# Attention with a transposed probability ring: order of the next head's reads, and which two tiles TensorE transposes

## The chip, the cores and the metric

The kernel runs on one core of one Trainium2 chip. The metric is the device time of one execution in microseconds. A core has TensorE (PE; its weight loads are listed apart as PEld), VectorE (DVE), ScalarE (ACT), GpSimd (POOL) and SyncE (SP). SP computes nothing here: it issues almost all DMA transfers, one after the other in the order of its own program. Sixteen DMA engines carry them.

## The reference

An adaLN-conditioned block: cached multi-head attention, then a small mixer and MLP. Only the attention is touched by the change. There are 32 heads of width 128, 2048 queries and 2048 keys, model width 640, all in bf16.

```python
def _A_ref(x, k_cache, v_cache, wq, wo):
    q = (x @ wq).reshape(B, Sq, H, Dh).transpose(0, 2, 1, 3)
    scores = jnp.einsum('bhqd,bhkd->bhqk', q, k_cache) * Dh ** (-0.5)
    p = _softmax(scores, axis=-1)
    o = jnp.einsum('bhqk,bhkd->bhqd', p, v_cache)
    return o.transpose(0, 2, 1, 3).reshape(B, Sq, H * Dh) @ wo

h = _layernorm(x) * (1 + ca) + sa
x = x + ga * _A_ref(h, A_k_cache, A_v_cache, A_wq, A_wo)
h = _layernorm(x) * (1 + cb) + sb
x = x + gb * _B_ref(h, B_w1, B_w2, B_w3, B_w4)
```

## The kernel before, in words

**Stages.** A start loads x, normalises it and makes its transpose `hT` in SBUF. The attention follows, one head after the other. The block's output projection, mixer and MLP come last; the change does not touch them.

**Tiles and steps.** A head's 2048 queries are 16 tiles of 128 rows. Tiles are numbered through all heads, g = 16 h + j, and one loop (L532) goes over steps s, one tile a step, with several stages of different tiles in one step. A tile meets these:

- Scores, `qk`, on PE (L286): two halves of 1024 keys, each of two matmuls, into the two halves of `Sps` in PSUM. A half can be written again only when DVE has read it.
- `negS` on DVE (L574): each half is scaled and copied to SBUF, with its row minimum. Two a tile.
- The exponential on ACT (L587), into slot s % 10 of the ring `Pb`. POOL (L584) joins the two minima before it.
- The transpose of the 128 x 2048 probabilities, so that keys lie on partitions, into `PTs`, also ten slots. It is done in one of two ways, below.
- The product with V, `pv`, on PE (L299), eight steps later (`PVD = 8`): two halves of eight matmuls. A half needs its half of `PTs`. After every second tile ACT copies the result (L565), POOL divides by the row sum and stores it to `o_scratch` by its own queue (L454).

**The two transposes.** Most tiles go through a DMA transpose from SP (`transpose`, L220 to L224): issued behind the exponential of an odd tile for a pair of tiles (1 MB), or for a tile alone (0.5 MB) where its neighbour isn't transposed so. Two tiles of each head, `PE_TILES`, are transposed on PE against an identity instead (`t_piece`, L253): four 128 x 128 pieces at a time, two halves r of eight pieces, into one of two PSUM banks (`JB`, in `Oaug` and `QPp`); then a copy to `PTs` (`t_evac`) by ACT (L262) or DVE (L264), as `by_dve` says. Half r of tile g is transposed in step g + 3 + r. With `PE_TILES = (3, 10)` the DMA transposes of a head are (0,1), 2, (4,5), (6,7), (8,9), 11, (12,13), (14,15).

**Projections.** The queries of head h + 1 are made during head h: four chunks of five matmuls (`q_piece`, L237), one matmul in a half-step, in the same two PSUM banks, each chunk copied by ACT (L244). `QPIECE` puts the chunks into half-steps that `taken` leaves free of transposing pieces; before, at half-steps 0 to 9 and 16 to 25 of 32.

**Order on PE in a step.** For each half: `qk`, then `pv` of tile s - 8, then a projection matmul or a transposing piece. PE works in this order, as every engine does in its own; waits are semaphores, worked out by the class `Prog` from what is read and written.

**Order on ACT and DVE in a step.** ACT: the copy of a pair's result, the copies of projections and of transposed halves, then the exponential. DVE: two `negS`, then a transposed half, where `by_dve` gives it one.

**Order on SP.** Behind a step's transpose come the reads for the following heads, into buffers that alternate by head: `load_k` (L205, a DMA transpose from the cache) at tile 2, `load_wq` (L209) at tile 6 for two heads on, `load_v` (L214) at tile 9. V's buffer for head h + 1 was last read by `pv` of the head before h, whose last tile is worked on in step 7 of head h. In the last head two reads of `o_scratch` (`load_ot`) for the output projection stand at tiles 2 and 9 instead.

Of the kernel before, what the change touches and what calls it, by code (L numbers as in the profile page):

```python
# [115 lines left out]
def bass_adaLN_cond__mha_block_cached__mixer_s_mlp__prompt_kernel(  # L116
# [3 lines left out]
    _, H, SK, DH = A_k_cache.shape  # L120
# [3 lines left out]
    NQT = SQ // 128  # L124
# [7 lines left out]
    NG = H * NQT  # L132
# [5 lines left out]
    with ExitStack() as es:  # L138
# [11 lines left out]
        if True:  # L150
            with ExitStack() as es1:
                sb1 = lambda name, shape, dt: es1.enter_context(nc.sbuf_tensor(name, shape, dt))
                RP = 10
                PVD = 8
                PE_TILES = (3, 10)
                US = KT * (SQ + 4)
                sb1("pad", [128, 32], F32)
                ring = sb1("ring", [128, 2 * RP, SK], BF16)
# [44 lines left out]
                def load_k(h):  # L203
                    hb = h % 2
                    G.dma("sync", lambda e: e.dma_start_transpose(KTs[:, hb], A_k_cache[0, h]), ("k", hb), w=[("KT", hb)])  # L205

                def load_wq(h):
                    hb = h % 2
                    G.dma("sync", lambda e: e.dma_start(wq[:, hb], A_wq[:, h * 128:(h + 1) * 128].rearrange("(k p) d -> p k d", p=128)),  # L209
                          ("wq", hb), w=[("wq", hb)])  # L210

                def load_v(h):
                    hb = h % 2
                    G.dma("sync", lambda e: e.dma_start(Vaug[:, hb, :, 0:128], A_v_cache[0, h].rearrange("(t p) d -> p t d", p=128)),  # L214
                          ("v", hb), w=[("V", hb)])

                assert RP % 2 == 0 and NQT % 2 == 0
                is_pe = lambda g: g % NQT in PE_TILES

# [8 lines left out]
                def bank(key):  # L228
                    if key not in bank_of:
                        bank_of[key] = jbank[0] % 2  # L230
                        jbank[0] += 1
                    return bank_of[key]
# [14 lines left out]
                def t_piece(g, r, q):  # L247
                    jb = bank(("t", g, r))

                    def f(t):  # L250
                        for z in range(4 * q, 4 * q + 4):
                            kt = 8 * r + z
                            ins = t.transpose(JBb[jb][:, z * 128:(z + 1) * 128], Pb[:, g % RP, kt * 128:(kt + 1) * 128], ident[:])  # L253
                        return ins
                    G.op("tensor", f, r=[("Pb", g % RP)], w=[("J", jb)])
# [7 lines left out]
                    else:  # L263
                        G.op("vector", lambda v: v.tensor_copy(dst, src), r=[("J", jb)], w=[("PT", g % RP, r)])  # L264

                by_dve = lambda g, r: r == 1 and g % NQT == PE_TILES[0]

                taken = [u for j in PE_TILES for u in range(2 * (j + 3), 2 * (j + 5))]
                QPIECE = {}
                u = 0  # L270
                for cc in range(NQC):
# [60 lines left out]
                if H > 1:  # L332
# [8 lines left out]
                     r=["id0"], w=["ident"])  # L341
# [3 lines left out]
                for k in range(KT):  # L345
                    G.op("gpsimd", lambda g, k=k: g.tensor_scalar(out=s_bc[:, k, :], in0=ones_f, scalar1=c_f[:, k:k + 1],
                                                                  scalar2=1.0, op0=ALU.mult, op1=ALU.mult),
                         r=["onesf", "cf"] + WRK, w=[("sbc", k)])
# [52 lines left out]
                def q_head0(cc):  # L401
                    for q in range(KT):
                        q_piece(0, cc, q)
                    q_evac(0, cc)
# [127 lines left out]
                for s in range(NG + PVD + LAG):  # L532
                    h, j = divmod(s, NQT)
                    g_ = s - PVD
                    evacs = []
                    if s <= 2:
                        for i in ((0,), (1, 2), range(3, len(MROW)))[s]:
                            mod_rows(i)
                    if s == 3:
                        G.op("gpsimd", lambda g: g.tensor_scalar(  # L540
                            out=mod_bc[:, 2 * D:3 * D], in0=mod_bc[:, 2 * D:3 * D], scalar1=1.0, scalar2=1.0, op0=ALU.add, op1=ALU.mult),
                            r=[("mod", i) for i in range(len(MROW))], w=["mod"])
                    for half in range(2):
                        if s < NG:
                            qk(s, half)
                        if half == 0 and s in (NG + PVD - 3, NG + PVD - 2):
                            b0 = a_pe(0, None if s == NG + PVD - 3 else b0, (s - NG - PVD + 3,))
                        if 0 <= g_ < NG:
                            pv(g_, half)
                        if s == 0 and half == 1:  # L550
                            q_head0(NQC - 1)
                        if h + 1 < H and 2 * j + half in QPIECE:
                            cc, q = QPIECE[2 * j + half]
                            q_piece(h + 1, cc, q)
                            if q == KT - 1:
                                evacs.append((q_evac, h + 1, cc))
                        for r in range(2):
                            g = s - 3 - r
                            if 0 <= g < NG and is_pe(g):
                                t_piece(g, r, half)  # L560
                                if half == 1:
                                    evacs.append((t_evac, g, r))
                    if 0 <= g_ < NG and g_ % 2 == 1:
                        p = g_ // 2
                        G.op("scalar", lambda a, p=p: a.copy(  # L565
                            Of[:, p % 4].rearrange("p z d -> p (z d)")[:, 0:259], PO[:, (p % 2) * 512:(p % 2) * 512 + 259]),
                            r=[("O", p % 2)], w=[("Of", p % 4)])
                    for fn, x, y in evacs:
                        if fn is q_evac or not by_dve(x, y):
                            fn(x, y)  # L570
                    for half in range(2):
                        if s < NG:
                            r8 = s % 8
                            G.op("vector", lambda v, half=half, s=s, r8=r8: v.tensor_scalar(  # L574
                                out=negS[:, s % 3, half * 1024:(half + 1) * 1024],
                                in0=Sps[:, half * 1024:(half + 1) * 1024],
                                scalar1=-SCALE, scalar2=None, op0=ALU.mult, op1=ALU.min,
                                accum_out=(nm0 if half == 0 else nm1)[:, r8:r8 + 1]),
                                r=[("S", half)], w=[("negS", s % 3), ("nmh", half, r8)])
                    for fn, x, y in evacs:  # L580
                        if fn is t_evac and by_dve(x, y):
                            fn(x, y)
                    if s < NG:
                        G.op("gpsimd", lambda g, r8=r8: g.tensor_scalar(  # L584
                            out=nm[:, r8:r8 + 1], in0=nm0[:, r8:r8 + 1], scalar1=nm1[:, r8:r8 + 1], scalar2=None, op0=ALU.min),
                            r=[("nmh", 0, r8), ("nmh", 1, r8)], w=[("nm", r8)])
                        G.op("scalar", lambda a, s=s, r8=r8: a.activation(  # L587
                            Pb[:, s % RP, :], negS[:, s % 3, :], ACT.Exp, bias=nm[:, r8:r8 + 1], scale=-1.0),
                            r=[("negS", s % 3), ("nm", r8)], w=[("Pb", s % RP)])
                        if not is_pe(s):  # L590
                            if s % 2 == 1 and not is_pe(s - 1):
                                transpose(s - 1, 2)
                            elif s % 2 == 1 or is_pe(s + 1):
                                transpose(s, 1)
                        if j == 2 and h >= 1 and h + 1 < H:
                            load_k(h + 1)
                        if h + 1 == H and j in (2, PVD + 1):
                            i = 0 if j == 2 else 1
                            load_ot(0, OTC[i], OTC[i + 1], i)
                        if j == 6 and h + 2 < H:  # L600
                            load_wq(h + 2)
                        if j == PVD + 1 and h + 1 < H:
                            load_v(h + 1)
                    if 0 <= s - PVD - LAG:
                        gr, z = divmod(s - PVD - LAG, 4)
                        if z == 0:
                            rcp(gr)
                        norm(gr, z)
                    if s == NG:
                        G.op("gpsimd", lambda g: g.memset(mhalf, -0.5), w=["mhalf"] + NEG)  # L610
                        load_ot(0, OTC[2], OTC[3], 2)
                        load_xt(0)
                        load_ot(1)
                    if s == NG + 2:
                        for cc in range(1, NQC):
                            load_xt(cc)
# [259 lines left out]
```

## Time and profile before

| what | value |
|---|---|
| three runs | 1611.37, 1616.06, 1617.12 us |
| the profiled execution, as timed | 1608.0 us |
| its span, first to last instruction | 1606.2 us |
| mean granted clock of TensorE | 0.993 |
| first `negS` of head 0, of head 3, of head 31 | 35.5, 151.7, 1221.1 us |
| L574, DVE `negS` half | 1024 times, 1221 ns each, 1178.6 us busy |
| L587, ACT exponential | 512 times, 2018 ns each, 1029.3 us busy |
| L299, PE product with V | 8192 matmuls, 647.5 us busy |
| L262, ACT copies of transposed halves | 96 times, 1021 ns (`Oaug`), 1013 ns (`QPp`) |
| DMA transposes of probabilities | 256 issues, 7.0 us from issue to landing (median) |
| reads of K, wq and V, 32 of each | 5.3, 3.4 and 5.0 us from issue to landing |

The span is the profiler's and the time is the run's own. A busy time is the union of a group's instructions; consecutive instructions of an engine may overlap a little, so the step from one to the next can be shorter than one's duration. "Idle before" is how long the engine had nothing to do before an instruction, with the instruction that ended the wait. A DMA row on SP lasts until SP can issue the next one; its landing comes later.

### The profile page before, as it was taken

The numbers are of one execution on the slowest core, as the hardware profiler recorded it, in microseconds if no ns is written. First come the engines' busy times: TensorE is split into PE (matmuls) and PEld (weight loads), VectorE is DVE, ScalarE is ACT, GpSimd is POOL, SyncE is SP. The second block draws the span as 40 slices with busy tenths as digits, with TensorE's granted clock in tenths as the row PEclk, the third lists the DMA queues.
The fourth block names the chain that finished last, engine by engine and source line by source line (L and its number), as shares of the span: only waits on it lengthen the run. The fifth ranks groups of instructions, "written<-read, shape, count | busy, mean of one in ns | idle before, by whom it ended". The sixth has DMA issues, their size and how long they took to land.

```text
span 1606.2 us, 34619 instructions
## 1 busy us (share of the span) xinstructions
PE 1488.3 (93%) x13978; PEld 961.6 (60%) x14231; DVE 1394.8 (87%) x2463; ACT 1294.5 (81%) x1145; POOL 625.0 (39%) x1394
## 2 busy tenths in 40 slices
PE   5899999989999999899999999999999799999999
PEld 3466666666666666666666666666666555545444
DVE  6999999999999999999999999999999366656425
ACT  4999999999999999999999999999999400055330
POOL 0244444444444444444444444444444333322000
PEclk9999999999999999999999999999999899999999
DMA  9999999999999999999999999999999995430000
GB/s 308 229 229 237 236 244 236 229 234 251 231 248 247 235 244 240 229 242 237 241 246 241 240 237 233 238 237 246 236 238 241 243 214 106 106 111 1 17 17 34
DMA packets 1167936, 333.60 MB, mean 208 GB/s; under 512 B 1148384, under 2 KB 1161760, under 8 KB 1167776
## 3 DMA queue, kind: packets, MB, share of 16 engines
q1 hardware_dynamic: 1161632, 314.59, 97.1%
q0 software_dynamic: 6144, 16.79, 3.7%
q8 instruction: 112, 1.84, 0.5%
q14 instruction: 48, 0.39, 0.1%
HBM read 43.48 MB, written 19.40 MB: 39 GB/s over the span
## 4 chain that ended last, share of the span: by engine, by line
DVE 36%; PE 22%; ACT 20%; DMA 12%; issue 9%; POOL 1%; POOLq 0%; DVEq 0%
DVE negS L574 33%; ACT ring L587 16%; DMA ring<-ring 12%; PE Sps L524 9%; PE Sps L806 4%; PE Oaug L757 2%; PE QPp L757 2%; ACT ring L262 2%; PE Sps L742 1%; PE PTp L299 1%; ACT kv L244 1%; DVE ring L264 1%; ACT Of L565 1%; PE Sps L286 1%; DVE ring L364 1%
## 5 line engine op out<-in xcount | busy, mean ns | idle before, releaser
L574 DVE TENSOR_SCALAR_CACHE_REDUCE negS<-Sps 128x1024 f32<-128x1024 f32 x1024 | 1178.6, 1221 | 30.0 <-PE Sps L286 29.3
L587 ACT ACTIVATE ring<-negS,small 128x2048 bf16<-128x2048 f32 x512 | 1029.3, 2018 | 22.3 <-POOL small L584 20.7
L299 PEld LDWEIGHTS PTp<-kv,ring 128*128 128x128 bf16 x8192 | 551.9, 98 | 313.9 <-DMA ring<-ring 100.8
L299 PE MATMUL PTp<-kv,ring 128*128 128x129 bf16 x8192 | 647.5, 221 | 52.5 <-DMA ring<-ring 51.8
L286 PE MATMUL Sps<-kv 128*128 128x512 bf16 x1950 | 592.5, 381 | 35.0 <-DVE negS L574 17.2
L584 POOL TENSOR_SCALAR small<-small 128x1 f32<-128x1 f32 x512 | 146.9, 287 | 628.4 <-DVE negS L574 628.3
L286 PEld LDWEIGHTS Sps<-kv 128*128 128x128 bf16 x2048 | 143.2, 97 | 139.4 <-DVE negS L574 94.9
L447 POOL TENSOR_SCALAR On<-Of,small 128x128 bf16<-128x128 f32 x512 | 191.6, 375 | 13.0
L440 POOL TENSOR_TENSOR small<-Of,small 128x4 f32<-128x4 f32 x128 | 133.2, 1041 | 14.6 <-ACT Of L565 14.5
L668 ACT COPY kv<-PTp 128x640 bf16<-128x640 bf16 x32 | 22.0, 692 | 141.1 <-PE PTp L665 141.1
L454 POOL DMA_DIRECT2D o_scratch<-On x128 | 103.1, 806 | 40.8 <-POOL On L447 37.2
L565 ACT COPY Of<-PTp 128x259 f32<-128x259 f32 x256 | 96.2, 376 | 19.6 <-PE PTp L299 19.6
L237 PE MATMUL Oaug<-hTx,kv 128*128 128x512 bf16 x264 | 100.4, 385 | 3.7 <-DVE hTx L396 3.7
L237 PE MATMUL QPp<-hTx,kv 128*128 128x512 bf16 x259 | 97.7, 382 | 2.7 <-ACT hTx L391 2.3
L574 DVE DVE_READ_ACCUMULATOR negS<-Sps 128x1 f32 x1024 | 86.2, 84 | 0.0
L624 POOL TENSOR_SCALAR negS<-negS 128x1 f32<-128x1 f32 x48 | 24.4, 508 | 143.9 <-DVE negS L633 143.9
L638 DVE TENSOR_TENSOR ring<-Sps,mod_bc 128x640 f32<-128x640 f32 x16 | 13.2, 824 | 72.8 <-PE Sps L524 72.8
L524 PE MATMUL Sps<-wo,hTx 128*128 128x512 bf16 (+1 forms) x503 | 70.5, 300 | 0.6 <-issue 0.2
L524 PE MATMUL Sps<-wo,negS 128*128 128x512 bf16 (+1 forms) x505 | 69.3, 298 | 0.4
L810 DVE TENSOR_TENSOR ring<-Sps,ring 128x640 f32<-128x640 f32 x15 | 12.4, 824 | 62.9 <-PE Sps L806 62.8
L262 ACT COPY ring<-Oaug 128x1024 bf16<-128x1024 bf16 x64 | 65.3, 1021 | 0.0
L524 PEld LDWEIGHTS Sps<-wo,hTx 128*128 128x128 bf16 x512 | 40.1, 99 | 31.2 <-issue 1.7
(88 smaller groups left out, 1008.8 us busy)
## 6 DMA issues: line engine op xcount, KB each, us to landing
kv<-in_A_v_cache_dram SPq DMA_DIRECT2D x32, 512.0 KB, 5.0
o_scratch<-On POOLq DMA_DIRECT2D x128, 128.0 KB, 3.8
ring<-in_A_x_dram SPq DMA_DIRECT2D x8, 640.0 KB, 6.4
kv<-in_A_wq_dram SPq DMA_DIRECT2D x32, 160.0 KB, 3.4
wo<-in_A_wo_dram SPq DMA_DIRECT2D x1, 5120.0 KB, 16.4
ring<-ring SPq DMA_TRANSPOSE x256, 7.0
ring<-in_w_mod_dram SPq DMA_DIRECT2D x1, 3200.0 KB, 13.0
out_dram<-wo SPq DMA_DIRECT2D x15, 160.0 KB, 1.8
```

Source lines behind the costliest of these rows:

```text
L237: G.op("tensor", lambda t: t.matmul(JB[jb], wq[:, hb, q, :], hT[:, q, cc * 512:(cc + 1) * 512], start=(q == 0), stop=(q == KT - 1)), r=[(" ...
L262: G.op("scalar", lambda a: a.copy(dst, src), r=[("J", jb)], w=[("PT", g % RP, r)])
L286: ins = t.matmul(Sps[:, col:col + 512], QT[:, hb, j * 128:(j + 1) * 128], KTs[:, hb, col:col + 512], start=True, stop=True)
L299: ins = t.matmul(ob[:, 0:129], PTs[:, b, kt, :], Vaug[:, hb, kt, 0:129], start=(kt == 0), stop=(kt == NKT - 1))
L440: G.op("gpsimd", lambda g: g.tensor_tensor(out=rl[:, 4 * b:4 * b + 4], in0=Of[:].rearrange("p a z d -> p (a z) d")[:, 4 * b:4 * b + 4, 128 ...
L447: G.op("gpsimd", lambda g: g.tensor_scalar(out=On[:, b, z, :], in0=Of[:, 2 * b + z // 2, z % 2, 0:128], scalar1=rl[:, 4 * b + z:4 * b + z ...
L454: G.dma("gpsimd", lambda e: e.dma_start(o_scr[jj // 2:jj // 2 + 2, :, hh].rearrange("a p z d -> p a (z d)"), On[:, b].rearrange("p (a z) d ...
L524: ins = t.matmul(YB[b][:, c0:c0 + cw], OTj[pr % 2][:, 2 * hh + z, :], wo[:, hh, c0:c0 + cw], start=(hh == 0), stop=(hh == H - 1))
L565: G.op("scalar", lambda a, p=p: a.copy(Of[:, p % 4].rearrange("p z d -> p (z d)")[:, 0:259], PO[:, (p % 2) * 512:(p % 2) * 512 + 259]), r= ...
L574: G.op("vector", lambda v, half=half, s=s, r8=r8: v.tensor_scalar(out=negS[:, s % 3, half * 1024:(half + 1) * 1024], in0=Sps[:, half * 102 ...
L584: G.op("gpsimd", lambda g, r8=r8: g.tensor_scalar(out=nm[:, r8:r8 + 1], in0=nm0[:, r8:r8 + 1], scalar1=nm1[:, r8:r8 + 1], scalar2=None, op ...
L587: G.op("scalar", lambda a, s=s, r8=r8: a.activation(Pb[:, s % RP, :], negS[:, s % 3, :], ACT.Exp, bias=nm[:, r8:r8 + 1], scale=-1.0), r=[( ...
```

## The change

Five edits, all in the attention.

- `PE_TILES` becomes a table from tile to offset: tile 8 is transposed in steps 11 and 12 (offset 3), tile 9 in steps 15 and 16 (offset 6), the latter being step 0 of the next head. `pv` of tile 9 comes in step 17. The DMA transposes of a head become (0,1), (2,3), (4,5), (6,7), (10,11), (12,13), (14,15).
- `taken` follows and wraps round the head's 32 half-steps: 22 to 25, 30, 31, 0 and 1. The projections then lie at half-steps 2 to 21.
- `by_dve`: of the four transposed halves of a head, DVE copies the second half of tile 8 in every head, and of tile 9 in odd heads. ACT copies the rest.
- K of the next head, wq of the one after and V of the next are read in this order behind the transpose of (6,7), at tile 7.
- In the last head the two reads of `o_scratch` stand at tiles 5 and 7.

```diff
-                PE_TILES = (3, 10)
+                PE_TILES = {8: 3, 9: 6}
...
-                by_dve = lambda g, r: r == 1 and g % NQT == PE_TILES[0]
-
-                taken = [u for j in PE_TILES for u in range(2 * (j + 3), 2 * (j + 5))]
+                by_dve = lambda g, r: r == 1 and (g % NQT == 8 or g // NQT % 2 == 1)
+
+                taken = [u % (2 * NQT) for j, o in PE_TILES.items() for u in range(2 * (j + o), 2 * (j + o + 2))]
...
                         for r in range(2):
-                            g = s - 3 - r
-                            if 0 <= g < NG and is_pe(g):
-                                t_piece(g, r, half)
-                                if half == 1:
-                                    evacs.append((t_evac, g, r))
+                            for o in PE_TILES.values():
+                                g = s - o - r
+                                if 0 <= g < NG and PE_TILES.get(g % NQT) == o:
+                                    t_piece(g, r, half)
+                                    if half == 1:
+                                        evacs.append((t_evac, g, r))
...
-                        if j == 2 and h >= 1 and h + 1 < H:
-                            load_k(h + 1)
-                        if h + 1 == H and j in (2, PVD + 1):
-                            i = 0 if j == 2 else 1
+                        if j == PVD - 1 and h + 1 < H:
+                            if h >= 1:
+                                load_k(h + 1)
+                            if h + 2 < H:
+                                load_wq(h + 2)
+                            load_v(h + 1)
+                        if h + 1 == H and j in (PVD - 3, PVD - 1):
+                            i = 0 if j == PVD - 3 else 1
                             load_ot(0, OTC[i], OTC[i + 1], i)
-                        if j == 6 and h + 2 < H:
-                            load_wq(h + 2)
-                        if j == PVD + 1 and h + 1 < H:
-                            load_v(h + 1)
```

## Prediction

> **What bounds the kernel now.** I read the page's head first: one profiled execution, span 1606.2 us, 1608.0 us as timed (1.8 us lie around the span). Runs gave 1611.37 to 1617.12, median 1616.06, so the profiled one is 8 us quicker than the median; I work out a difference against 1606.2 and carry it to the median.
>
> ```profile
> span 1606.2 us, 34619 instructions
> PE 1488.3 (93%) x13978; PEld 961.6 (60%) x14231; DVE 1394.8 (87%) x2463; ACT 1294.5 (81%) x1145; POOL 625.0 (39%) x1394
> ...
> DVE 36%; PE 22%; ACT 20%; DMA 12%; issue 9%; POOL 1%; POOLq 0%; DVEq 0%
> ...
> L264 DVE COPY ring<-QPp 128x1024 bf16<-128x1024 bf16 x32 | 22.0, 687 | 0.0
> ```
>
> Four engines are near full, and the chain hops among them, so shares settle nothing. Next the busy time by stretch, for heads 3 to 30 (from the first L574 of head 3 to that of head 31):
>
> ```profile
> core 0: us, PE busy (x) PEld busy (x) DVE busy (x) ACT busy (x) POOL busy (x), PEclk, DMA share, GB/s
> 151.70:1221.10 1069.40, 1001.47 (x10227) 681.56 (x10414) 1046.38 (x1821) 1049.37 (x868) 490.07 (x1120) 1.00 1.20 239
> ```
>
> 28 heads in 1069.4 us are 38.19 us a head. DVE alone would need less: its rows L574 follow each other every 1.144 us, so 32 x 1.144 = 36.61 us a head, plus 0.60 for the one copy L264 (its row says 687 ns, but 0.60 is how much later the next L574 starts): **37.21**. So 0.95 to 0.98 us a head are lost, and the lines of L222 with the waits of DVE say to whom:
>
> ```profile
> L222 SPq DMA_TRANSPOSE ring<-ring x225: 1637/4330/6447, 149.7 to 1218.4; - x113
> ...
>   PE PTp L299: 42.9, 64
> ...
> DMA to landing us min/median/max: 3.9/7.1/9.0
> ...
> DVE negS L574 <- PE Sps L286: 22.5, 40, 1.6
> ```
>
> PE waits for transposes 64 times in 28 heads, then gives DVE its scores late. Why are they late? SP's queue in time, head 17:
>
> ```profile
> 645.99 21.11 SPq L222 DMA_TRANSPOSE ring<-ring  x5
> 667.15 2.33 SPq L205 DMA_TRANSPOSE kv<-in_A_k_cache_dram  x1
> 669.52 4.47 SPq L222 DMA_TRANSPOSE ring<-ring  x1
> 674.03 0.59 SPq L209 DMA_DIRECT2D kv<-in_A_wq_dram  x1
> 674.67 9.48 SPq L222 DMA_TRANSPOSE ring<-ring  x2
> 684.19 0.58 SPq L214 DMA_DIRECT2D kv<-in_A_v_cache_dram  x1
> 684.82 3.77 SPq L222 DMA_TRANSPOSE ring<-ring  x1
> ```
>
> Each row starts where the last one ends. Following the records one by one (heads 3 to 29), every transpose row starts 2.1 us or more after the exponential that feeds it has ended: the queue never waits for data. **The transfers set the pace**, one after the other. From landing to landing they take on the mean: (0,1) 4.91, 2 alone 2.30, K 2.94, (4,5) 4.53, wq 0.79, (6,7) 4.38, (8,9) 4.42, V 2.71, 11 alone 2.37, (12,13) 4.21, (14,15) 4.62: 38.16 us, the head's period. DVE stands 0.95 us below it.
>
> **The change part by part, per head.**
>
> Seven pairs. Two singles (2.30 + 2.37 = 4.67) become a pair, the bytes stay. All pairs: mean 4.51, so 0.16 saved. Many intervals hold an instruction fetch (queues 8 and 14): with one a pair takes 5.4, without 3.87, a single 2.15 without; so 0.43 in calm. Bounds: clean pairs at (8,9) and (12,13) take 3.67, the clean singles 2.25 and 2.03, so 0.61 at best; at worst, were SP's own issuing the pace, the shortest pair row (4.0) against two of the shortest single (1.64) would lose 0.7. Since SP's rows stretch with the landings, I take the calm 0.43.
>
> The Trainium skill ("DMA: Bandwidth & Descriptors", section on the anatomy of one DMA, whose fit is for the GpSimd path) gives every transfer a fixed 2.0 us or so beside its bytes; by that one transfer fewer saves 2.0 us. The trace differs: singles land 2.3 us apart although each takes several us from issue to landing, so the fixed part lies under the transfer before.
>
> K, wq and V together. Nothing is added, each is only moved on SP: K behind (4,5) and (6,7), wq behind (6,7), V ahead of the next pair. Today plain reads break the row of transposes twice, then once. The pair behind wq takes 4.02 in calm against 3.67, so 0.35 to be had at best, 0 at worst; I take 0.17. V's wait for the last PV of the head before (step 7) is over when SP reaches it, about 11 us after exponential 7; if not, pair (10,11) is behind it and PE would stand at tile 2 of the next head. The stretch costs 2.94 + 0.79 + 2.71 = 6.4, with (6,7) 10.9, against four steps of 2.38 = 9.5 until tiles 10 and 11 are there; the other six pairs need 4.5 of 4.76 each and win that back. The queue's delay then swings by some 1.3 us below today's 4.1, so it does not run dry (2.8 remain). K lands about 12.6 us after exponential 7 ends, some 2.5 us before PE wants it: cover enough, though thin.
>
> So the transfers' floor is 38.16 - 0.43 - 0.17 = **37.56**, between 37.2 and 38.9.
>
> Copies. Today each head has 3 on ACT, 1 on DVE. After: even heads 3 and 1, odd heads 2 and 2; 48 on DVE, 80 on ACT. DVE gains 0.60 every second head: 37.21 + 0.30 = 37.51. ACT loses 16 copies of 1.02 us; it is not the limit (its rows L587 idle for POOL, 0.6 us a head), so I count that nothing.
>
> Tile 9, transposed by PE at steps 15 and 16 and used at step 17. Today a copy is done four steps ahead of its PV. Now, on even heads, the second half is copied by ACT between exponentials 15 and 16, one step ahead. The same two copies in a row exist today, tile 10's at steps 13 and 14 (head 14):
>
> ```profile
> 606.81 1.22 DVE L574 TENSOR_SCALAR_CACHE_REDUCE negS<-Sps 128x1024 f32<-128x1024 f32 x1 [0.39 <-PE Sps L286]
> ...
> 608.45 1.01 ACT L262 COPY ring<-QPp 128x1024 bf16<-128x1024 bf16 x1
> ...
> 608.63 0.63 PE L299 MATMUL PTp<-kv,ring 128*128 128x129 bf16 x8
> ...
> 610.25 1.22 DVE L574 TENSOR_SCALAR_CACHE_REDUCE negS<-Sps 128x1024 f32<-128x1024 f32 x1
> ```
>
> The copy ends at 609.46; the PV half that would need it started at 608.63. It would wait 0.83 us. From the start of such a PV half to the next L574 is 1.33 us (619.38 to 620.71), so that L574 would start at 610.84 and not 610.25: 0.6 us of DVE lost. Worked from ACT's own steps (0.27 for Of, 0.91 for a copy, 1.90 for an exponential, against DVE's 2.29 a tile) the copy ends 1.74 us after the tile's last L574, 0.3 later: 0.9. I take 0.75 every second head, 0.38. On odd heads DVE copies right behind its tile, ready about when PE comes: nothing. Bounds of this term: 0 (hidden by PE's spare half us) and 1.0 (below). Projections move to half-steps 2 to 21 in one row; 28 of 32 half-steps carry an extra piece as before: nothing, PE's heavy half-step of 1.11 us being under DVE's 1.144. The last head's two transposed reads of `o_scratch` move among the same transfers, and its end hangs on their sum: nothing; uncovered, each would show as 3.5 us.
>
> DVE's floor: 37.51 + 0.38 = **37.89**. It is now the higher one. As they lie close, chance waits of either cost a little, 0.06 by my choice: 37.95 a head, 0.21 less than 38.16. Heads 3 to 31, 29 of them: -6.1 us. Heads 1 and 2 ran at 37.22 and 37.30 before the queue had filled; they now pay DVE's floor: +1.3. Sum **-4.8 us**: 1601.4 span, 1603.2 timed, and 1611 against the median.
>
> **Rivals.**
>
> *Faster, DVE alone decides.* Both savings come whole (37.2) and PE's spare time hides tile 9's copy: 37.51 a head, 29 x -0.65 + 0.5 = -18 us, 1598. For it: clean pairs of 3.67. Against: the copy at 609.46. By the skill's fixed 2.0 us the transfers would fall to 36.2, and this rival's result would be the same, DVE being next; the trace bears that price out nowhere.
>
> *Slower, tile 9's copy on ACT.* ACT starts an exponential 1.3 us after its tile's scores at tile 15 on the mean, 2.4 at most. Where it runs at that maximum on even heads, the copy comes 1.1 us later than in the 0.9 case: 2.0 lost, 1.0 a head, DVE's floor 38.51; 29 x 0.35 + 2.6 = +13 us, 1629. It decides once more than 1.9 us are lost per even head. Against: tiles 13 and 14 leave ACT no extra work, so it should be 0.4 behind.
>
> *The transfers stay as they are.* Merging and moving win nothing (fetches make up for it): 38.16, 0 to +2 us, 1616 to 1618.
>
> **How the numbers follow.** About 0.5% (8 us) is what a measurement tells from no change. The forecast of -5 us 0.34, the unchanged transfers 0.08: same 0.42. Faster rival and all between it and the forecast beyond 8 us: 0.36. Slower: 0.22. The likeliest case's own range is 1605 to 1619; for 8 in 10 it reaches to the edge of the faster rival and close to the slower: 1599 to 1628.
>
> **What would show it.** 224 transposes; L262 80 and L264 48 times. Landings of the pairs near 4.5, the sum of a head's transfers under 37.8, SP's rows now and then starting right at an exponential's end. PE's L299 waiting for ACT L262 at tile 1 behind even heads, 0.6 to 1.0 us, and none behind odd ones. Periods of 38.0 in both kinds of head. It is wrong if transposes still keep DVE waiting 0.9 us a head, if K or V is waited for, or if tile 9's copy costs over 1.9.

## The result and the profile after

| | before | after |
|---|---|---|
| median | 1611.97 us | 1618.90 us |
| lowest to highest | 1605.56 to 1620.48 | 1611.03 to 1625.93 |
| the profiled execution as timed | 1608.0 | 1623.46 |
| its span | 1606.2 | 1621.6 |
| a head, heads 3 to 30 of the profile | 38.19 | 38.63 |

The changed kernel takes 1.0043 times as long, 95% interval 1.0031 to 1.0056: 6.9 us more between the medians, where 4.8 us less were forecast. The two profiled executions lie on opposite sides of their medians (3.97 us under it before, 4.56 over it after), so their spans differ by 15.4 us, and about 8.5 of these belong to the draw (which executions happened to be profiled) and not to the change. Of the 15.4, 1.4 us arise before head 3 begins (1.3 were forecast there), 12.2 in the 28 heads and 1.8 after them. The heads' figures below come from these two executions, so about half of the 0.44 us that a head has gained there is the draw's too.

The page's head, its chain and two of its groups, after:

```profile
span 1621.6 us, 34763 instructions
...
DVE 42%; PE 22%; DMA 14%; ACT 12%; issue 8%; POOL 1%; SPq 0%; POOLq 0%
...
L575 DVE TENSOR_SCALAR_CACHE_REDUCE negS<-Sps 128x1024 f32<-128x1024 f32 x1024 | 1180.0, 1220 | 37.3 <-PE Sps L286 36.8
...
L262 ACT COPY ring<-Oaug 128x1024 bf16<-128x1024 bf16 x64 | 65.1, 1017 | 0.0
```

(Below the diff the lines are one higher: L575 was L574, L588 was L587.) The chain has moved from ACT to DVE, 36% to 42% and 20% to 12%: DVE was indeed brought near the bound. Next the same stretch as in the prediction, heads 3 to 30, with the same columns, and three rows of its waits (us, times, longest):

```profile
153.07:1234.74 1081.67, 1016.53 (x10420) 689.96 (x10418) 1055.06 (x1835) 1046.16 (x855) 490.45 (x1120) 1.00 1.21 236
```

```profile
DVE negS L575 <- PE Sps L286: 26.1, 40, 1.4
...
PE PTp L299 <- DMA ring<-ring: 22.2, 40, 1.6
...
PE PTp L299 <- ACT ring L262: 16.8, 14, 1.2
```

The stretch is 12.2 us longer than before, while DVE's busy time rose by only 8.7 (14 copies of 0.62). DVE is idle 26.6 us of it, where it was 23.0. PE's product with V now waits for two things: for transposes 40 times, and for ACT's copy 14 times, once behind every even head, for 1.2 us. The late copy of tile 9 is this one, here behind head 16 (columns: start, us, engine, line, and in brackets the idle time before it and what ended it):

```profile
695.39 1.22 DVE L575 TENSOR_SCALAR_CACHE_REDUCE negS<-Sps 128x1024 f32<-128x1024 f32 x1
...
696.27 1.01 ACT L262 COPY ring<-QPp 128x1024 bf16<-128x1024 bf16 x1
...
697.34 0.64 PE L299 MATMUL PTp<-kv,ring 128*128 128x129 bf16 x8 [1.20 <-ACT ring L262]
...
698.66 1.22 DVE L575 TENSOR_SCALAR_CACHE_REDUCE negS<-Sps 128x1024 f32<-128x1024 f32 x1 [0.91 <-PE Sps L286]
```

ACT's copy ends at 697.28 and PE starts at 697.34; DVE's next tile starts 2.13 us after the one before it (696.53), instead of 1.144: 0.99 lost, the same in each even head. Behind odd heads DVE makes that copy, and the next tile starts 0.60 later, without a wait.

SP's queue in head 16:

```profile
683.82 2.71 SPq L205 DMA_TRANSPOSE kv<-in_A_k_cache_dram  x1
686.58 0.59 SPq L209 DMA_DIRECT2D kv<-in_A_wq_dram  x1
687.21 1.57 SPq L214 DMA_DIRECT2D kv<-in_A_v_cache_dram  x1
688.83 16.03 SPq L222 DMA_TRANSPOSE ring<-ring  x3
```

The rows still follow each other without a gap, and in the records every transpose row of heads 3 to 29 starts at least 0.63 us after the exponential that feeds it: the queue never ran empty. From landing to landing: (0,1) 5.33, (2,3) 4.19, (4,5) 5.21, (6,7) 4.58, K 2.60, wq 1.02, V 2.65, (10,11) 4.33, (12,13) 4.47, (14,15) 4.28. That sums to 38.66. The three reads take 6.27 where they took 6.44, the 0.17 that was forecast. The seven pairs take 32.39 where six pairs and two singles took 31.74: 0.65 more in this execution, not 0.43 less.

### The profile page after: what moved, and what is told of

The parts are those of the page before. It is cut to its first block, busy times and chain, and to the rows that moved or that the text cites. A ratio compares the mean times of both kernels' runs of the same rounds, so it can differ in the third digit from the quotient of the medians.

```text
span 1621.6 us, 34763 instructions
## 1 busy us (share of the span) xinstructions
PE 1509.8 (93%) x14231; PEld 969.9 (60%) x14231; DVE 1404.8 (87%) x2479; ACT 1290.4 (80%) x1129; POOL 624.8 (39%) x1394
## 3 DMA queue, kind: packets, MB, share of 16 engines
q8 instruction: 112, 1.84, 0.5%
## 4 chain that ended last, share of the span: by engine, by line
DVE 42%; PE 22%; DMA 14%; ACT 12%; issue 8%; POOL 1%; SPq 0%; POOLq 0%
DVE negS L575 39%; DMA ring<-ring 13%; ACT ring L588 8%; PE Sps L524 7%; PE Sps L807 4%; PE PTp L299 2%; PE Oaug L758 2%; PE QPp L758 2%; ACT ring L262 2%; DVE ring L264 2%; PE Sps L743 1%; PE Sps L286 1%; DMA hTx<-o_scratch 1%; DVE ring L364 1%; POOL small L585 1%
## 5 line engine op out<-in xcount | busy, mean ns | idle before, releaser
L575 DVE TENSOR_SCALAR_CACHE_REDUCE negS<-Sps 128x1024 f32<-128x1024 f32 x1024 | 1180.0, 1220 | 37.3 <-PE Sps L286 36.8
L588 ACT ACTIVATE ring<-negS,small 128x2048 bf16<-128x2048 f32 x512 | 1018.3, 2006 | 44.2 <-POOL small L585 38.6
L286 PE MATMUL Sps<-kv 128*128 128x512 bf16 x2048 | 612.8, 381 | 33.8 <-DVE negS L575 28.2
L286 PEld LDWEIGHTS Sps<-kv 128*128 128x128 bf16 x2048 | 155.9, 97 | 146.8 <-DVE negS L575 93.0
L237 PE MATMUL Oaug<-hTx,kv 128*128 128x512 bf16 x320 | 121.6, 385 | 2.9 <-ACT hTx L391 2.1
L237 PE MATMUL QPp<-hTx,kv 128*128 128x512 bf16 x320 | 120.7, 381 | 2.7 <-ACT hTx L391 2.3
L566 ACT COPY Of<-PTp 128x259 f32<-128x259 f32 x256 | 92.3, 360 | 13.9 <-PE PTp L299 13.9
L575 DVE DVE_READ_ACCUMULATOR negS<-Sps 128x1 f32 x1024 | 85.0, 83 | 0.0
L524 PE MATMUL Sps<-wo,hTx 128*128 128x128 bf16 (+1 forms) x512 | 72.7, 303 | 2.9 <-DMA hTx<-o_scratch 2.9
L524 PE MATMUL Sps<-wo,negS 128*128 128x128 bf16 (+1 forms) x512 | 70.7, 299 | 0.0
L262 ACT COPY ring<-Oaug 128x1024 bf16<-128x1024 bf16 x64 | 65.1, 1017 | 0.0
```

The lines of the kernel that those rows point to most:

```text
L237: G.op("tensor", lambda t: t.matmul(JB[jb], wq[:, hb, q, :], hT[:, q, cc * 512:(cc + 1) * 512], start=(q == 0), stop=(q == KT - 1)), r=[(" ...
L262: G.op("scalar", lambda a: a.copy(dst, src), r=[("J", jb)], w=[("PT", g % RP, r)])
L286: ins = t.matmul(Sps[:, col:col + 512], QT[:, hb, j * 128:(j + 1) * 128], KTs[:, hb, col:col + 512], start=True, stop=True)
L524: ins = t.matmul(YB[b][:, c0:c0 + cw], OTj[pr % 2][:, 2 * hh + z, :], wo[:, hh, c0:c0 + cw], start=(hh == 0), stop=(hh == H - 1))
L566: G.op("scalar", lambda a, p=p: a.copy(Of[:, p % 4].rearrange("p z d -> p (z d)")[:, 0:259], PO[:, (p % 2) * 512:(p % 2) * 512 + 259]), r= ...
L588: G.op("scalar", lambda a, s=s, r8=r8: a.activation(Pb[:, s % RP, :], negS[:, s % 3, :], ACT.Exp, bias=nm[:, r8:r8 + 1], scale=-1.0), r=[( ...
```

## The experiments

Every ratio is to the kernel before on the same chip, with its 95% interval. Figures for a head are those of one profiled execution, heads 3 to 30. "DVE's own sum" is what a head would take if DVE never waited for a transpose: 36.61 + 0.60 for each copy it makes + 0.99 where tile 9's copy is late on ACT. For the changed kernel: 36.61 + 0.60 + (0.60 + 0.99)/2 = 38.01.

### First: the late copy, the stretch, or the copies?

**Tile 9 one step earlier** (its second copy is then two steps ahead of its use):

```diff
-                PE_TILES = {8: 3, 9: 6}
+                PE_TILES = {8: 3, 9: 5}
```

> The changed kernel with tile 9 transposed one step earlier (offset 5: steps 14 and 15; the projections move to half-steps 0 to 19), so its second half is copied two steps ahead of its product with V; copies still alternate by head. Theory A (the late copy of tile 9, 0.99 us of DVE on even heads, is what costs): that stall is gone, DVE needs 37.5 us a head, the head's period falls from 38.6 to between 37.6 and 38.1, ratio to before 0.992 to 0.999. Theory B (the transfers themselves became slower, 38.66 us a head from landing to landing, through seven pairs or the reads in one stretch): period stays 38.6, ratio 1.003 to 1.006.

Measured: 1.0024 [1.0010, 1.0038], median 1613.50, between the two theories; the interval overlaps that of the changed kernel (1.0031 to 1.0056). The stall behind even heads is gone. A head still takes 38.52 us in the profile, and PE's wait for transposes is up from 22.2 to 34.3 us (49 times). The 0.5 us a head that DVE no longer loses to the copy it now loses mostly to late transposes.

**The same, with one copy a head on DVE** (as before the change):

```diff
-                PE_TILES = {8: 3, 9: 6}
+                PE_TILES = {8: 3, 9: 5}
...
-                by_dve = lambda g, r: r == 1 and (g % NQT == 8 or g // NQT % 2 == 1)
+                by_dve = lambda g, r: r == 1 and g % NQT == 8
```

> As the one before, and DVE copies one transposed half per head (tile 8's second) in every head, ACT three. DVE then needs 37.2 us a head as in the kernel before. Theory A: 0.990 to 0.998, at or below the version with alternating copies. Theory B: 1.003 to 1.006, the copies being of no account. If ACT's third copy matters, it is slower than the alternating version.

Measured: 0.9989 [0.9973, 1.0005], median 1608.15, again between the theories. Against the kernel ahead of it, on the same chip, the alternation of the copies alone is gone, and 0.35% with it. Windows and two waits, heads 3 to 30:

```profile
151.13:1220.84 1069.71, 1013.47 (x10419) 694.30 (x10416) 1046.58 (x1823) 1048.70 (x869) 488.13 (x1120) 1.00 1.22 240
```

```profile
PE PTp L299 <- DMA ring<-ring: 34.7, 51, 2.6
DVE negS L575 <- PE Sps L286: 22.4, 39, 2.7
```

38.20 us a head, although DVE's own sum is 37.21, and SP's queue never runs empty: here the transfers set the pace, as before, and their landings sum to 38.11: 31.7 us for the seven pairs and 6.4 for the three reads, which is what six pairs, two singles and the reads took before. This is the transfers' floor with seven pairs and one stretch, measured where DVE's sum lies 0.99 us under the pace. The prediction had it at 37.56.

**The stretch alone**, in the kernel before:

```diff
-                        if j == 2 and h >= 1 and h + 1 < H:
-                            load_k(h + 1)
+                        if j == PVD - 1 and h + 1 < H:
+                            if h >= 1:
+                                load_k(h + 1)
+                            if h + 2 < H:
+                                load_wq(h + 2)
+                            load_v(h + 1)
...
-                        if j == 6 and h + 2 < H:
-                            load_wq(h + 2)
-                        if j == PVD + 1 and h + 1 < H:
-                            load_v(h + 1)
```

> The kernel before with one edit: K, wq and V read in this order behind the transpose of tiles 6 and 7. Tiles 3 and 10 stay with TensorE, copies as before. Theory A: the stretch is harmless or saves some 0.2 us a head, ratio 0.994 to 1.001. Theory B, stretch: it is what slows the transfers, ratio 1.003 to 1.010.

Measured: 1.0337 [1.0308, 1.0366], median 1663.06, far over both theories. Its row of waits:

```profile
DVE negS L574 <- PE Sps L286: 73.0, 52, 3.4
```

Here pair (8,9) stands right behind the three reads, lands late in every head, and DVE stands about 2.6 us at tile 0 of the next one. SP then waits for exponentials elsewhere: the queue has room, but at the wrong place. In the changed kernel tiles 8 and 9, which need no transfer, leave a gap in the row there, and neither K nor V was waited for. So the stretch can't be judged without PE's tiles.

**The reads apart again**, in the changed kernel:

```diff
-                        if j == PVD - 1 and h + 1 < H:
-                            if h >= 1:
-                                load_k(h + 1)
-                            if h + 2 < H:
-                                load_wq(h + 2)
+                        if j == 3 and h >= 1 and h + 1 < H:
+                            load_k(h + 1)
+                        if j == 6 and h + 2 < H:
+                            load_wq(h + 2)
+                        if j == PVD + 1 and h + 1 < H:
                             load_v(h + 1)
```

> The changed kernel with the reads apart: K behind (2,3), wq between (4,5) and (6,7), V at tile 9 in the gap without transposes. Theory A: the late copy stays, ratio 1.003 to 1.006 or a little more. Theory B, stretch: the ratio comes back to 1.000. Theory B, pairs: stays at 1.004.

Measured: 0.9986 [0.9964, 1.0008], median 1607.44. With the same copies on DVE and the same late copy on ACT, most heads alternate between 37.8 and 38.2 us, which is DVE's own sum without and with the late copy, and SP now waits for exponentials (within 0.1 us of their end at (0,1), (2,3), (10,11) and (14,15) in 16 to 23 of 27 heads). A few heads of 39.4 to 41.1, where (4,5) is late behind K, bring its profile to a mean of 38.48; this execution took 7.15 us more than its kernel's median. So the copies' price isn't owed everywhere.

### Second: which of the parts loses it

**One DVE copy, tile 9 earlier, reads apart** (the edits of "one copy a head" and of "the reads apart" together):

```diff
-                PE_TILES = {8: 3, 9: 6}
+                PE_TILES = {8: 3, 9: 5}
...
+                by_dve = lambda g, r: r == 1 and g % NQT == 8
...
+                        if j == 3 and h >= 1 and h + 1 < H:
+                            load_k(h + 1)
```

> Tiles 8 and 9 on TensorE with offsets 3 and 5, DVE copies one half a head, and the reads apart (K at tile 3, wq at 6, V at 9): DVE needs 37.2 us a head, so the transfers show what they need with the reads apart. Theory A (seven pairs save what was worked out, and the stretch gives it back): period 37.3 to 37.8, ratio 0.984 to 0.994. Theory B (seven pairs need 38 us wherever the reads stand): 0.997 to 1.002, as off5_one (0.9989).

Measured: 0.9988 [0.9970, 1.0006], median 1609.69, 38.27 a head. DVE's own sum of 37.21 isn't reached here either: no gain from both remedies at once. Here SP's queue does run empty at (10,11) and (14,15) in about half of the heads.

**V read only for the first two heads** (a later head's V isn't read), in the changed kernel:

```diff
-                            load_v(h + 1)
+                            if h == 0:
+                                load_v(h + 1)
```

> The changed kernel, reading V for the first two heads only (the later heads' reads of V are left out): the transfers lose some 2.7 us a head and cannot be the limit. What is left is the sum on DVE: 36.6 + 0.6 (tile 8) + 0.99 or 0.60 (tile 9, even or odd heads) = 38.0. If that limit holds, periods alternate about 38.0, ratio 0.993 to 0.998. If the late copy and the copies on DVE cost less than that, 37.2 to 37.6 and a ratio under 0.988. If PE is the limit, 38.3 or more.

Measured: 0.9943 [0.9926, 0.9960], median 1600.49, and 38.02 a head: DVE's own sum of 38.01, now that the transfers are some 2.6 us shorter. The DVE half of the prediction's sum stands, 0.12 over its 37.89.

**One DVE copy a head, tile 9 late in every head**, in the changed kernel:

```diff
-                by_dve = lambda g, r: r == 1 and (g % NQT == 8 or g // NQT % 2 == 1)
+                by_dve = lambda g, r: r == 1 and g % NQT == 8
```

> The changed kernel with only tile 8's second half copied by DVE, so tile 9's comes late from ACT in every head. If the late copy costs 0.99 us of DVE each time and the copy on DVE 0.60: the sum on DVE is 38.2 a head, 0.2 over the changed kernel's, ratio 1.004 to 1.010. If the copies on DVE are what costs: under 1.003.

Measured: 1.0001 [0.9989, 1.0013], median 1610.18. Its waits, and SP in head 16:

```profile
PE PTp L299 <- ACT ring L262: 33.5, 28, 1.2
...
PE PTp L299 <- DMA ring<-ring: 1.7, 5, 0.5
```

```profile
680.80 0.53 SPq L214 DMA_DIRECT2D kv<-in_A_v_cache_dram  x1
682.67 16.36 SPq L222 DMA_TRANSPOSE ring<-ring  x3
```

Now every head pays the 0.99, DVE's own sum is 38.20, higher than the changed kernel's 38.01, and nearly every head takes just that. Transposes are hardly ever late (1.7 us against 22.2). Between 681.33 and 682.67 SP waits for its exponential: the queue runs empty. A kernel with the higher DVE sum is 0.42% faster. What the change loses therefore isn't the height of DVE's sum, nor the late copy by itself: it goes away with the alternation of the copies alone.

**The alternation alone**, in the kernel before:

```diff
-                by_dve = lambda g, r: r == 1 and g % NQT == PE_TILES[0]
+                by_dve = lambda g, r: r == 1 and (g % NQT == 3 or g // NQT % 2 == 1)
```

> The kernel before with DVE copying also tile 10's second half in odd heads: DVE needs 37.5 instead of 37.2 us a head, the transfers stay at 38.2. If the larger limit alone decides: 0.998 to 1.002. If two limits lying near each other add up: 1.003 to 1.008.

Measured: 1.0043 [1.0028, 1.0058], median 1616.76, 38.48 a head. That is as large as the whole loss of the change, with none of its other parts, and with DVE's own sum (37.51) 0.65 us under the pace of the transfers.

### Third: DVE's time, or ACT's relief?

**The copy twice**: in odd heads of the kernel before, DVE makes tile 3's copy a second time; ACT's work stays.

```diff
+                        if g // NQT % 2 == 1:
+                            G.op("vector", lambda v: v.tensor_copy(dst, src), r=[("J", jb), ("PT", g % RP, r)], w=[("PT", g % RP, r)])
```

> The kernel before, where in odd heads DVE makes tile 3's copy twice (the same data to the same place, the second behind the first). DVE gains 0.6 to 0.7 us every second head, as in b_copies, but ACT's work and tile 10 stay as they were. Theory D (any time on DVE shows, though the transfers' queue is never empty): ratio 1.003 to 1.006 as b_copies. Theory E (it was taking tile 10's copy from ACT, or its place at tile 14): 0.999 to 1.001.

Measured: 1.0040 [1.0024, 1.0055], median 1619.11, 38.47 a head. The same loss, so it is DVE's time in every second head that costs (0.69 us a copy by its busy time: 9.7 us more in 14 heads), not what ACT no longer does.

**All copies on ACT**, in the kernel before:

```diff
-                by_dve = lambda g, r: r == 1 and g % NQT == PE_TILES[0]
+                by_dve = lambda g, r: False
```

> The kernel before with all four copies of a head on ACT. DVE needs 36.6 us a head (0.6 less), ACT 38.1 (0.9 more). Theory D and ACT not limiting: 0.990 to 0.995. If the transfers alone set the pace: 0.999 to 1.001. If ACT becomes the limit: 1.000 to 1.004.

Measured: 0.9993 [0.9975, 1.0012], median 1611.26. DVE is relieved by 0.6 a head and nothing is won: ACT is then busy 38.17 of each head's 38.39 us, and has become the bound.

**Every DMA transpose a single**, in the kernel before (14 a head for 8):

```diff
-                            if s % 2 == 1 and not is_pe(s - 1):
-                                transpose(s - 1, 2)
-                            elif s % 2 == 1 or is_pe(s + 1):
-                                transpose(s, 1)
+                            transpose(s, 1)
```

> The kernel before with every DMA transpose of one tile: 14 transfers a head in place of 8, same bytes. If a transfer more costs 0.4 us, as the prediction took for a merge: 6 x 0.43 = 2.6 us a head, ratio 1.04 to 1.05. If merging is worth nothing: 0.99 to 1.005. By a fixed 2 us for each transfer: 1.2 and more.

Measured: 1.0335 [1.0305, 1.0364], median 1667.02, 40.03 a head: 1.84 us for six transfers more, 0.31 each, some of it a TensorE clock below full in four places. One transfer fewer should thus be worth about 0.3, near the 0.43 that was taken and within its bounds; the ratio lies between what 0.43 and what nothing would give. The Trainium skill's fixed 2.0 us a transfer ("DMA: Bandwidth & Descriptors", section on the anatomy of one DMA, a fit for the GpSimd path) would make the six 12 us, as an estimate; for transposes queued behind each other on SP the run shows 1.84.

**V later**, on top of tile 9 earlier and one DVE copy:

```diff
+                        if j == 13 and h + 1 < H:
                             load_v(h + 1)
```

> off5_one with V read behind (12,13) and only K and wq in the gap of tiles 8 and 9. If the bunching of the three reads ahead of (10,11) costs: below 0.995 (0.9989 for off5_one). If only the sum of a head's transfers counts: 0.997 to 1.001.

Measured: 0.9972 [0.9955, 0.9990], median 1608.71, 38.16 a head. It is the only complete kernel here whose interval lies under 1, and so the one that beats both; by 0.3%, which is little with this many kernels compared.

### Fourth: what DVE's time does, with the queue full

**The second copy on one partition of 128**, otherwise as the copy twice:

```diff
+                            G.op("vector", lambda v: v.tensor_copy(dst[0:1], src[0:1]), r=[("J", jb), ("PT", g % RP, r)], w=[("PT", g % RP, r)])
```

> b_twice with the second copy cut to one partition of 128: about the same time on DVE, hardly any data. Theory D1 (time on DVE adds to the head): 1.003 to 1.005, as b_twice. Theory D2 (the copy's reads and writes slow the transfers): 0.999 to 1.001.

Measured: 1.0055 [1.0035, 1.0075], median 1620.34. As dear as the full copy, with next to none of its traffic and about its time (679 ns for 691): it is the time on DVE, not the bytes in memory. The second copy also holds its PSUM bank longer; no run takes that apart from DVE's time, but the alternation alone holds none longer and loses as much.

**The copy twice in every head**: the same line without the `if`.

> b_twice in every head: 0.65 us more on DVE per head, its sum 37.9 against the transfers' 38.2. Theory D1, in proportion: 1.007 to 1.010. If the larger sum decided after all and b_twice's price came from heads taking turns: 0.999 to 1.003.

Measured: 1.0066 [1.0047, 1.0086], median 1622.72, 38.69 a head. Some 22 us were put on DVE (32 times 0.69) and 10.2 came out; with the copy twice in every second head 11 were put in and 6.4 came out. What comes out isn't in proportion: the ratio falls between the two theories.

**V read only for the first two heads**, in the kernel before (later heads' V isn't read):

```diff
-                        if j == PVD + 1 and h + 1 < H:
+                        if j == PVD + 1 and h == 0:
```

> The kernel before, reading V for the first two heads only (later reads of V left out): the transfers lose 2.7 us a head, 35.5. If nothing but the transfers stands between the kernel and DVE's sum: 37.2 us a head, 1 us less, ratio 0.980 to 0.984. If something else holds it back: above 0.986.

Measured: 0.9801 [0.9771, 0.9830], median 1581.00. The group of L574 on its page:

```profile
L574 DVE TENSOR_SCALAR_CACHE_REDUCE negS<-Sps 128x1024 f32<-128x1024 f32 x1024 | 1175.5, 1239 | 6.9 <-PE Sps L286 6.5 <-ACT ring L587 0.2
```

DVE waits 6.9 us in all for this group, against 37.3 in the changed kernel's row, and a head takes 37.24, DVE's own sum of 37.21. The reading of the profile before holds: the transfers set its pace, and DVE stands 0.95 us under it.

## Why the prediction was wrong, point by point

**What bounded the kernel: right.** Without V's read the kernel before falls to 37.24, the 37.21 that was read from the rows of L574.

**The late copy of tile 9: right in mechanism and place, a little dearer.** Forecast 0.75 every second head, measured 0.99, at tile 1 behind even heads, none behind odd ones. DVE's floor of 37.89 became 38.01, which the changed kernel without V's reads takes (38.02). The slower rival, over 1.9 lost per even head, didn't come.

**K, wq and V in one stretch: right in that nothing is added; the saving isn't shown.** They took 6.27 us for 6.44, and neither K nor V was waited for. But the same stretch took 6.43 with tile 9 earlier and one DVE copy, so the 0.17 may be this execution's luck. What was missed is how much the place matters: with a pair that needs landing soon behind them, the same reads cost 3.4%.

**Seven pairs, "the transfers' floor is 37.56": this step failed.** The term is the 0.43 for two singles made a pair, with the 0.17 for the stretch. Measured where DVE's sum lies well under, the floor is 38.1: both together saved 0.05. The mean prices had given 0.16 for the merge, and the prediction chose the price of undisturbed transfers. That price holds: without a fetch between its landing and the one before, a pair takes 3.95 (3.89 before), with no store either 3.68 (3.67 before), and a transfer more costs 0.31. What failed is that a head isn't undisturbed. In the packet records, undisturbed stretches move 290 GB/s. Counted in slices of 0.1 us, this is what a head loses against that rate, in us:

| where | before | changed | tile 9 earlier, one DVE copy | alternation alone | copy twice |
|---|---|---|---|---|---|
| around instruction fetches | 5.28 | 5.93 | 5.70 | 5.32 | 5.53 |
| around stores to `o_scratch` | 1.54 | 1.68 | 1.63 | 1.86 | 1.60 |
| where one transfer hands over to the next | 1.98 | 1.63 | 1.38 | 1.92 | 1.95 |
| sum, with nothing lost elsewhere | 8.80 | 9.24 | 8.71 | 9.10 | 9.07 |

("Around" is from 0.3 us ahead of a fetch to 2.0 behind its end, from 0.1 ahead of a store to 0.2 behind its end, and from 1.5 ahead of a landing to 0.6 behind it; a slice counts for the first that fits. The executions of the first and the third column lie equally far under their medians, 4 us, so these two compare best.) With one DVE copy and tile 9 earlier the hand-overs shrank by 0.60, as much as was taken for both terms, but 0.42 of it came back around fetches and 0.09 around stores. The fetches themselves are as many in all five (119 or 120 in the 28 heads). The third rival ("fetches make up for it", 38.16) had named this, and got a chance of 0.08. Why a fetch costs more behind pairs alone isn't settled; with the reads apart 5.35 is lost around them, with tile 9 late in every head 5.29. SP's own issuing isn't the pace: its shortest row at each place adds up to 33.2 us a head in the changed kernel.

**"The higher of the two floors decides", with 0.06 for closeness: this step failed too, and it sets the sign.** With a transfers' floor of 38.1 in place of 37.56 the same rule would have given 38.1 to 38.2 a head, no change. That came true for the two kernels that keep the stretch and have one DVE copy a head (1.0001 and 0.9989). The alternating copies put 0.30 a head on DVE, 9.6 us in 32 heads, and 6 to 7 of these came out at the end, in the changed kernel as in the kernel before, though a full queue should have hidden them. The step's price was 0.06 a head; it measured about 0.22 (6.9 us over the 31 heads from head 1 on).

**How the loss is to be understood, as far as the runs go.** Three pairs of kernels differ only in whether DVE makes one more copy in every second head, and each time these cost about as much: 1.0001 and 1.0043, 0.9989 and 1.0024, 1 and 1.0043. The loss shows when DVE's sum lies within some 0.7 us of a queue that never runs empty (after the change, the alternation alone, the copy twice). It is gone when the queue gets slack: reads apart (0.9986), DVE's steady 38.20 (1.0001). It is smaller when tile 9's copy is no longer late (1.0024), though the intervals overlap. The same list of transfers, in the same order, landed in 38.66 us in the changed kernel and in 38.11 with tile 9 earlier and one DVE copy. Only the work on tile 9 (PE's step, and who copies it) and the half-steps of the projections differ. About half of these 0.55 us is the draw of the two executions (4.56 over its median, 3.99 under); the ratios leave about 0.28. So here the transfers' floor wasn't a constant to be compared with DVE's: it moved with DVE's work. **By which path it moved stays open.** The thin copy rules out DVE's traffic, and the copy twice rules out ACT's relief. Nor is it one place in the table: with the alternation alone the loss stands around stores (1.86 for 1.54), with the copy twice around fetches (5.53 for 5.28).

**Copies off ACT: nothing, as forecast.** The copy twice leaves ACT its work and loses the same.

**The last head.** 1.8 us of the spans' difference lie behind the 28 heads; no run took that part apart, and it is less than one execution differs from another.

**Counts and signs.** 224 transposes, L264 48 times and L262 80 times (64 in the row above, 16 out of QPp) came as foretold, and the waits for ACT at tile 1 too (1.2 us where 0.6 to 1.0 were given). Periods of 38.0 and a queue that now and then runs dry did not; at (10,11) the least margin was 0.63 us and the mean 1.8, where 2.8 were given. That 1618.90 lies between 1599 and 1628 is luck and that range's width: the time went to the other side of no change, and not by the late copy that the slower rival had feared. "Transposes still keep DVE waiting 0.9 us a head" was to be the sign of failure: it is 0.62 in this execution (38.63 - 38.01) after 0.98 before (38.19 - 37.21), where the forecast had left 0.06.

## What to carry to other kernels

Before a saving in transfers is counted as lower floor, look at what disturbs them: where instruction fetches and stores take a few us of a head, merging transfers changes what these cost, and the undisturbed prices aren't what comes out. Two limits within 2% of each other are not safely combined by taking the higher: here work put on the lower one showed at half to seven tenths of its length, and a kernel with the higher but steady floor, whose queue gets slack, can be the faster. A read that is moved is judged by the transfer that stands right behind it and by when that has to land.

## What the runs showed of the hardware

**Instruction fetches.** The queues of the changed kernel, 148 to 1240 us (packets, MB, share of 16 engines):

```profile
q8 instruction: 83, 1.36, 0.5%
```

About three packets of 16 KB a head, 1.0 us each at the median, 0.5% of the 16 DMA engines' time. Yet a pair with a fetch in it lands 5.4 us after the transfer before it and one that nothing disturbs 3.7. Of the 5.9 us a head lost around fetches, some 1.7 would be lost there anyway at the rate of the rest of the time, so as an estimate 0.5% of the engines' time costs over 4 of 38 us. A transfer's landing is the last of its sixteen counts in the records, so one late count makes it late. The Trainium skill ("DMA: Bandwidth & Descriptors", section on queues, rings and completion order) says that an engine drains a whole packet of one queue before it turns to the next; a packet of 1.0 us in front of rows of 256 bytes agrees with that, though 1.7 us is more than it explains.

**A short wait can halve TensorE's clock.** PE in the kernel with the stretch alone, behind a wait of 1.77 us:

```profile
641.73 0.99 PE L299 MATMUL PTp<-kv,ring 128*128 128x129 bf16 x8 [1.77 <-DMA ring<-ring]
...
642.94 1.06 PE L286 MATMUL Sps<-kv 128*128 128x512 bf16 x2
643.79 1.07 PE L299 MATMUL PTp<-kv,ring 128*128 128x129 bf16 x8
...
645.60 0.63 PE L299 MATMUL PTp<-kv,ring 128*128 128x129 bf16 x8
```

The same instructions take 1.07 and 0.63 us; the granted clock between 641.60 and 645.00 is 0.53. Such a stretch follows the stall in 19 of that kernel's 28 heads, and makes a late transpose dearer than its wait. The Trainium skill ("TensorE: Matmul & The Clock Gate", section on what is happening) gives an idle window of about 3.4 us for it; here a wait of 1.77 us was enough, and the slow stretch is about that window long. Not every such wait does it: behind one of 1.84 us in the same kernel (838.6 us), and of 2.07 with every transpose a single (1040.3 us), the granted clock stayed at 1.
